# Attention, soft MoE and maxout on one core: another order of emission for all parts of a pair of heads

## The chip, the cores and the metric

The kernel runs on one core of a Trainium2 chip. The metric is the time of one execution on the device in microseconds, the median of several. The engines of a core run side by side, each through its own list of instructions in order: TensorE (PE in the profile; its weight loads are PEld), VectorE (DVE), ScalarE (ACT), GpSimd (POOL) and SyncE (SP), which here issues all DMA transfers.

## The reference

The inputs are q, k and v of 4 batches x 8 heads x 576 positions x 64, all in float32. Three layers follow each other:

```python
q_rot, k_rot = rotate(q), rotate(k)                    # rotary embedding
scores = q_rot @ k_rot.T / 8                           # 576 x 576 per head
attn = softmax(scores)                                 # exp(scores - row max) / row sum
x = (attn @ v) as [2304, 512]
logits = x @ phi                                       # 32 slots
slot_input = softmax(logits over all 2304 rows).T @ x  # soft mixture of experts
slot_out = relu(slot_input @ w1[e]) @ w2[e]            # 8 experts, 512 -> 1024 -> 512
y = softmax(logits over the slots) @ slot_out
h = max(y @ w1, y @ w2, y @ w3)                        # maxout, 512 -> 768
out = h @ w_out
```

## The kernel before

The 32 heads are worked through as 16 pairs (g = 0 to 15). A pair has nine units of up to 128 rows of scores: units 0, 2, 4, 6 belong to one head, 1, 3, 5, 7 to the other, and unit 8 holds the last 64 rows of both. Each unit runs through a chain over three engines. `emit_S` (PE, line 354; 342 in the first pair) computes the scores into one of three PSUM banks of the pool `ps_s`. `emit_max` (DVE, line 359) takes the row maximum. `emit_exp` (ACT, line 371) writes the exponentials to SBUF and their row sums. `emit_T` (PE, lines 380 to 386) transposes them back into the unit's bank, and `emit_Te` copies them out (ACT, lines 403 and 405; for unit 8 DVE, lines 408 and 411). Only then is the bank free for another S. So at most three units are on their way at once. Unit 8 has eight S matmuls, the others four.

`emit_PV` (PE, lines 430 and 433) multiplies them by v in two groups of five steps, PV0 (units 0 to 3) and PV1 (units 4 to 8), c0 to c4 each. Both accumulate in the one bank of the pool `ps_u`; `emit_u` reads it, first on ACT (called uhi here, line 442), then on DVE (ulo, line 440). `emit_x` (line 471) multiplies by the identity and by phi on PE, `emit_xe` (DVE, line 488) divides by the row sums of `emit_den`, `emit_lg` sums the logits. After each fourth pair `emit_end` adds the batch to the slot inputs (PE matmuls of lines 527, 541 and 556).

Ahead of S, a pair is prepared some two pairs earlier: loads of q, k and v (`load_qk`, `load_v`, `load_vr`), the rotation on POOL (`emit_rope`, parts q, k, r), transposes on PE into the bank of `ps_m` (`emit_qk`, called qk-q, qk-k, qk-r), a copy on ACT, the remainder of the split on DVE (`emit_lo`: lo-q, lo-k, lor), and DMAs within SBUF that lay the parts out (`emit_stack`, line 303, four DMAs each for q and k). Between all this runs a conversion of the last layer's weights from float64 bits to float32 (`convert`, 32 chunks in four steps each): DVE lines 610, 613, 615 and 618, with ACT lines 596 and 620 and POOL lines 622 and 624 in or after the fourth step. A `fill` is one step; `store` and `load_raw` on SP belong to the first step of a chunk. `emit_xr` splits phi, in the first pair.

The order is written out by hand, as numbers. Each part has a time in the table `TIMES`, counted in units; part X of pair g is put at 9 g + X. The events are sorted by that number, and each engine's list is the sorted list's part for that engine:

```python
for _, _, f, a in sorted(ev, key=lambda e: e[:2]):
    f(*a)
```

`first` replaces the times of the units in pair 0 and of the preparation of pair 1; `last` has those of the parts of pair 15 behind the units. In pair 15 the second PV group is split: a narrow part (y = 1, tile ul, the 64 last positions of both heads) and a wide one (y = 0).

The expert weights (32 loads of 1 MB, `load_w`, line 150) come into SBUF as space is free: ten during pairs 1 to 10, the other 22 behind the last conversion, where `swap` frees one pool after another (the working space of load, rotation and conversion; of the stacks; of S; of exp, T, Te and PV0; of PV1; of the rest) and later ones as the expert matmuls (line 742) have used the earlier ones.

Of the kernel before, what the change touches and what calls it, by code (L numbers as in the profile page):

```python
# [15 lines left out]

TIMES = {'PV0': [6.052698, 6.539022, 6.831161, 7.041179, 8.370574],
# [4 lines left out]
 'den': 9.045966,  # L24
 'dveT': [8],
 'end': [15.996553, 16.470809, 18.107722, 18.802385],
 'exp': [-0.675131, -0.916498, -1.127766, -0.304154, -0.913015, -1.011578, -0.953932, -0.243716, -1.040539],
 'fill': [-1.316643, 0.146837, 0.779834, 0.899125, 1.252142, 4.242488, 5.036954, 5.844713, 6.810021, 7.369609],
 'fill0': [-2.965317, 1.274402, 1.506862, 5.137451, -0.677174, 3.405875, 5.934943],
 'fillb': [0.263554, 0.659419, 1.262914, 4.782657, 7.03104],  # L30
# [3 lines left out]
           'exp': [-7.893717, -27.924269, -6.082201, -4.622187, -0.966764, -1.860446, -1.972664, 0.213131, -0.679221],  # L34
           'lok': -6.168845,
           'loq': -22.133635,
           'lor': -13.346412,
           'max': [-1.919995, 40.189116, -13.728982, -6.819962, -1.88512, -1.867328, -2.393284, -1.184347, -1.911995],
           'qkk': -8.826648,
           'qkq': -23.658995,  # L40
           'qkr': -13.35598,
           'stackk': -5.63826,
           'stackq': -11.947606},
 'h': [0, 0, 0.5, 1.5, 2, 2, 3.5, 4, 5.5, 5.0, 6.0, 6.5, 9.0, 10, 12.5, 18, 18.5, 24.0, 32.5, 40, 39, 44.5, 45, 51, 57, 58, 60.0, 68.0,
       71.5, 76.5],
 'hact': [[2, 2], [2, 5], [2, 1], [0, 5]],
 'last': {'PV1': [13.362323, 23.757612, 27.866613, 32.577903, 34.487854],
          'PV1b': [9.034314, 9.623589, 9.670028, 10.656968, 11.314749],
          'den': [12.059624, 7.065112],
          'end': [15.553272, 40.986824, 53.411692, 75.731423],  # L50
          'endb': [111.764265, 112.019026, 114.008368, 119.095903],
          'lg': [14.02684, 62.06959],
          'u1': [35.240849, 35.241849],
          'u1b': [29.443596, 31.049719],
          'warm': [[57.500286, 4], [57.655604, 4], [97.595993, 4]],
          'x': [11.566386, 42.509109, 34.56566],
          'xe': [[12.445342, 30.186802], [51.307524, 53.750567], [57.173325, 55.473275]]},
 'lg': [15.366289],
 'loadqk': -22.678765,
 'loadr': -22.34179,  # L60
 'loadv': -1.873124,
 'loadw': 15.022565,
 'lok': -7.015135,
 'loq': -11.030046,
 'lor': -9.491336,
 'max': [-1.11053, -1.080468, -1.701921, -1.209456, -0.992138, -1.336195, -0.990138, -0.989138, -1.184604],
 'onact': [1, 0, 0],
 'qkk': -8.083624,
 'qkq': -12.675556,
 'qkr': -10.180993,  # L70
 'ropek': -16.364586,
 'ropeq': -17.904547,
 'roper': -14.747196,
 'stackk': -6.992883,
 'stackq': -8.503989,
 'u0': [8.703314, 8.807017],
 'u1': [10.743395, 11.315174],
 'warm': [0, 0],
 'warm0': [24, 18, 5, 6],
 'warme': 3,  # L80
 'x': [11.5668, 12.630236, 13.065397],
 'xe': [12.623938, 14.727613, 13.993235],
 'xr': [-13.461787, -1.717465, -3.018039, 1.372009],
 'xu': [0, 1, 0]}


# [1 line left out]
def tile_kernel(ctx, tc, q, k, v, phi, w1, w2, g1, g2, g3, wo, rope, out):  # L88
# [45 lines left out]
    def slot(i, shape, dtype, name):  # L134

        if i == NW - 1:
            return late.tile(shape, dtype, tag="xy", name=name)
        pool = next(p for n, p in reversed(wpools) if i >= n)
        return pool.tile(shape, dtype, tag=f"w{i}", name=name)
# [248 lines left out]
    def emit_Te(n):  # L388
# [11 lines left out]
        src = s.rearrange("p b c -> p (b c)").rearrange("p (c i) -> p c i", i=128)  # L400
        copy = nc.vector.tensor_copy if j in TIMES["dveT"] else nc.scalar.copy
        if x == 0:
# [58 lines left out]
    def emit_x(g, ts):  # L461
# [4 lines left out]
        else:  # L466
            pool, tag = (ps_u, "u") if TIMES["xu"][ts[0] // 2] else (ps_m, "m")
            ps = pool.tile([128, 512], F32, tag=tag, name=f"x{g}_{ts[0]}")
# [38 lines left out]
    def warm(n, pool, tag, first):  # L507

        w = pool.tile([128, 2, 512], F32, tag=tag, name=f"warm{tag}") if first else run["warm"]
        run["warm"] = w  # L510
        for _ in range(n):
            nc.tensor.transpose(w[:, 0, 0:128], ident, ident)

    def emit_end(b, step, t0=0, t1=5):

        pool, tag = (ps_u, "u") if t0 else (ps_m, "m")
        if t0 and step in (2, 3):
            warm(TIMES["warme"], ps_s, "s", False)
        if step:
# [109 lines left out]

    WT = TIMES['warm']  # L630
    def emit_tail():
# [193 lines left out]
        def emit_h(k, f, part=(0, 1)):  # L825
# [14 lines left out]
            h = slot((6, 7, 13, 14)[i % 4], [128, 512], F32, f"hf{k}_{f}")[:, 0:n]  # L840
            if [k, f] in TIMES["hact"]:

# [38 lines left out]

        rows = sorted((t, i) for i, t in enumerate(TIMES["h"]) if i > 1)
        step = 0
# [215 lines left out]
```

## Time and profile before

| | |
|---|---|
| time, 3 runs | median 487.65 us (487.19 to 489.44) |
| span of the profiled execution | 486.8 us; the page gives no time of its own for it, the median lies 0.85 us above |
| PE, PEld, DVE, ACT, POOL busy | 466.3, 347.8, 345.4, 294.4, 282.6 us |
| pairs of heads | up to about 339 us, 18.6 to 21.3 us each |
| chain that ended last | PE 62%, DMA 13%, DVE 9%, ACT 8% of the span |
| DMA | 105.67 MB, mean 217 GB/s |

Read it from the stage and not from the shares: PE's busy time is modelled and includes what it waits inside an instruction, so the question is always which instruction starts late and who released it. A row of the timeline merges equal instructions that follow each other; the difference of two starts is what the first took, the printed length also holds the pipeline's depth. A row of the windows gives the stretch, its length, and the busy time with the number of instructions of PE, PEld, DVE, ACT and POOL in this order.

### The profile page before, as it was taken

The page shows a single profiled execution, that of the slowest core. Times are in us where ns is not written, and L with a number is a line of the kernel's source. Part 1 is how long each engine was busy: PE and PEld are TensorE (multiplying, and loading weights), DVE is VectorE, ACT ScalarE, POOL GpSimd, SP SyncE. Part 2 cuts the span into 40 slices and gives each one's busy share as a digit, 9 for nine tenths or more (in the row PEclk, how much of TensorE's full clock was granted, in tenths as well). Part 3 has the DMA queues.
Part 4 walks back from the last instruction along what each step waited for, and adds up shares of the span by engine and source line. Part 5 has one row for each costly group of instructions (what it writes and reads, how often), then busy time and mean ns, then how long its engine had stood idle before and what let it go on. Part 6 is the DMA issues. An engine that isn't in the chain of part 4 may idle for free.

```text
span 486.8 us, 9778 instructions
## 1 busy us (share of the span) xinstructions
PE 466.3 (96%) x3392; PEld 347.8 (71%) x3392; DVE 345.4 (71%) x663; ACT 294.4 (60%) x652; POOL 282.6 (58%) x374
## 2 busy tenths in 40 slices
PE   7899998999999999999999999998999899999996
PEld 7778676787777877868768687774334567888885
DVE  7878997987889898799988898466321367545520
ACT  2778887786978787788788688661111445322311
POOL 5998879777698796769976753011000287423420
PEclk9999999999999999999999999999999999999999
DMA  8679799979999998999989647999999501111111
GB/s 219 165 205 229 193 266 268 292 193 251 278 259 277 254 266 240 231 254 302 262 239 231 171 117 174 295 367 390 386 386 406 224 0 45 65 44 65 43 66 65
DMA packets 73121, 105.67 MB, mean 217 GB/s; under 512 B 12144, under 2 KB 41456, under 8 KB 72560
## 3 DMA queue, kind: packets, MB, share of 16 engines
q1 hardware_dynamic: 73072, 105.04, 73.8%
q8 instruction: 27, 0.44, 0.4%
q14 instruction: 22, 0.18, 0.1%
HBM read 66.98 MB, written 11.01 MB: 160 GB/s over the span
## 4 chain that ended last, share of the span: by engine, by line
PE 62%; DMA 13%; DVE 9%; ACT 8%; issue 3%; POOL 3%; SPq 2%; ACTq 0%; DVEq 0%; POOLq 0%
PE r L898 14%; PE s L354 11%; PE u L430 10%; PE s L380 9%; DMA qst<-qkt 3%; PE h L742 3%; DMA wof<-wod 3%; PE g L838 3%; ACT P L371 3%; PE u L433 2%; DMA kst<-qkt 2%; PE x L471 2%; DVE hf L847 2%; DMA wmd<-cv 2%; SPq L768 1%
## 5 line engine op out<-in xcount | busy, mean ns | idle before, releaser
L359 DVE TENSOR_REDUCE nm<-s 128x1 f32<-128x576 f32 x144 | 108.0, 750 | 18.4 <-PE s L354 15.7
L371 ACT ACTIVATE P<-s,nm 128x576 f32<-128x576 f32 x144 | 107.2, 745 | 14.6 <-DVE nm L359 13.1
L354 PE MATMUL s<-kst,qst 128*128 128x288 f32 x600 | 109.2, 312 | 3.0 <-ACT pt L403 1.6
L354 PEld LDWEIGHTS s<-kst,qst 128*128 128x128 f32 x600 | 84.3, 189 | 13.8 <-issue 6.8
L380 PE MATMUL s<-ident,P 128*128 128x128 f32 x576 | 90.9, 280 | 1.5 <-ACT P L371 1.3
L380 PEld LDWEIGHTS s<-ident,P 128*128 128x128 f32 x576 | 63.8, 140 | 25.1 <-ACT P L371 13.8
L898 PE MATMUL r<-wo,h 128*128 128x512 f32 x324 | 78.6, 391 | 0.4 <-ACT ob L862 0.2
L430 PE MATMUL u<-pt,vn 128*64 128x256 f32 (+1 forms) x512 | 72.0, 413 | 0.1
L898 PEld LDWEIGHTS r<-wo,h 128*128 128x128 f32 x324 | 60.3, 188 | 14.6 <-POOL h L858 0.9
L847 DVE TENSOR_REDUCE hf<-g 128x512 f32<-128x1536 f32 (+1 forms) x26 | 40.9, 1600 | 27.0 <-PE g L838 22.8
L858 POOL TENSOR_TENSOR h<-hf,h 128x512 fp32r<-128x512 f32 (+1 forms) x30 | 35.4, 1181 | 41.3 <-ACT h L857 41.1
L403 ACT COPY pt<-s 128x512 f32<-128x512 f32 x64 | 37.5, 587 | 26.7 <-PE s L380 25.5
L405 ACT COPY pt<-s 128x640 f32<-128x640 f32 x64 | 44.6, 697 | 8.0 <-PE s L382 7.6
L622 POOL TENSOR_TENSOR raw<-raw 128x384 f32<-128x384 f32 x32 | 27.1, 848 | 37.2 <-ACT raw L620 31.3
L430 PEld LDWEIGHTS u<-pt,vn 128*64 128x64 f32 x512 | 32.5, 136 | 22.4 <-issue 5.1
L857 ACT CAST h<-hf 128x512 fp32r<-128x512 f32 (+1 forms) x30 | 17.3, 578 | 48.2 <-DVE hf L847 42.8
L710 POOL TENSOR_TENSOR wo<-wof,wo 128x512 fp32r<-128x512 f32 x6 | 7.7, 1282 | 46.3 <-ACT wo L709 46.3
L624 POOL TENSOR_TENSOR cv<-cv,raw 128x384 f32<-128x384 f32 x32 | 32.7, 1023 | 2.5
L371 ACT ACTIVATION_READ_ACCUMULATOR P<-s,nm 128x1 f32 x144 | 28.9, 201 | 0.0
L615 DVE SCALAR_TENSOR_TENSOR cv<-raw,cv 128x384 uint32<-128x384 uint32 x32 | 27.5, 859 | 0.4
L471 PE MATMUL x<-xr,ut 128*128 128x256 f32 x160 | 26.4, 294 | 0.3 <-DVE qkt L297 0.3
L610 DVE TENSOR_SCALAR cx<-cv 128x384 f32<-128x384 f32 x32 | 17.5, 547 | 7.8 <-ACT cv L596 7.6
(363 smaller groups left out, 765.7 us busy)
## 6 DMA issues: line engine op xcount, KB each, us to landing
wt<-in_moe_w_dram SPq DMA_DIRECT2D x32, 1024.0 KB, 10.1
qst<-qkt SPq DMA_DIRECT2D x60, 288.0 KB, 6.2
raw<-in_moe_w_dram SPq DMA_DIRECT2D x24, 384.0 KB, 5.8
kst<-qkt SPq DMA_DIRECT2D x30, 160.0 KB, 5.1
wmd<-cv SPq DMA_DIRECT2D x24, 192.0 KB, 4.0
kst<-qkt SPq DMA_DIRECT2D x30, 144.0 KB, 5.2
vn<-in_v_dram SPq DMA_DIRECT2D x16, 256.0 KB, 6.8
wm<-wmd SPq DMA_DIRECT2D x4, 1024.0 KB, 14.2
```

Of the source, the lines that this page charges most:

```text
L354: nc.tensor.matmul(s[:, h, 0:288], l, r[:, 288 * h:288 * h + 288], start=(i == 0), stop=(i == len(todo) - 1))
L359: nc.vector.tensor_reduce(out=nm[n], in_=st[n][:, :, 0:288], axis=AX.XY, op=ALU.max, negate=True)
L371: nc.scalar.activation(out=dst.rearrange("p (h c) -> p h c", h=2), in_=s[:, :, 0:288], func=AF.Exp, bias=nm.pop(n), accum_out=acc)
L380: nc.tensor.transpose(s[:, 0, 128 * c:128 * c + 128], p[:, c0 + 128 * c:c0 + 128 * c + 128], ident)
L403: copy(out=o[:, 0:4, w + q0:w + q0 + 128], in_=src[:, 0:4, :])
L405: copy(out=o[:, 0:5, q0:q0 + 128], in_=src[:, 0:5, :])
L430: nc.tensor.matmul(u[r, 0:q1 - q0], vn[g][:, x, 64 * c:64 * c + 64], o[:, c, c0 + q0:c0 + q1], start=(c == 0), stop=False)
L471: nc.tensor.matmul(ps[:, 256 * i:256 * i + 256], utf[:, S * z + 128 * t:S * z + 128 * t + 128], xr[:, 0:hp + 2:hp + 1, :], start=(z == 0), ...
L624: nc.gpsimd.tensor_tensor(out=t3, in0=t3, in1=hf, op=ALU.add)
L847: nc.vector.tensor_reduce(out=h, in_=ps[:, :, 0:n].rearrange("p m n -> p n m"), axis=AX.X, op=ALU.max)
L858: nc.gpsimd.tensor_tensor(out=lo, in0=h, in1=hi.bitcast(F32), op=ALU.subtract)
L898: nc.tensor.matmul(p, a[:, s_], w, start=(z0 == 0 and z == 0), stop=(z0 == NF - 1 and z == 2))
```

## The change

Nearly all numbers of `TIMES` are others; no line of code beside the table is changed. The times of the tail (`h`, `hact`, the warming matmuls) are as they were.

```diff
- 'PV1': [9.241587, 9.242837, 9.546836, 10.367914, 10.622399],
- 'S': [-1.309708, -1.59755, -2.545633, -1.884619, -1.490997, -2.22163, -1.388557, -1.487997, -2.474781],
+ 'PV1': [9.714536, 9.714736, 9.714936, 9.715136, 9.715336],
+ 'S': [-1.74769, -1.606214, -2.189842, -1.701744, -1.95565, -2.08495, -1.560098, -1.975774, -3.300465],
...
- 'fill': [-1.316643, 0.146837, 0.779834, 0.899125, 1.252142, 4.242488, 5.036954, 5.844713, 6.810021, 7.369609],
+ 'fill': [-1.50987, 0.004675, 0.220815, 3.698955, 0.656176, 7.194923, 7.843254, 0.689867, 4.548494, 5.293259],
...
- 'first': {'S': [-3.975538, -2.669185, -21.686737, -6.89008, -7.669434, -2.602921, -2.632212, -1.578422, -2.027835],
+ 'first': {'S': [-3.975538, -2.669185, -57.562865, -12.285873, -18.031466, -15.122047, -2.687969, -5.348835, -8.984009],
...
- 'last': {'PV1': [13.362323, 23.757612, 27.866613, 32.577903, 34.487854],
-          'PV1b': [9.034314, 9.623589, 9.670028, 10.656968, 11.314749],
+ 'last': {'PV1': [25.832191, 26.930466, 26.930666, 26.930866, 26.931066],
+          'PV1b': [8.641384, 15.657113, 12.981078, 10.937847, 25.762469],
...
- 'loadv': -1.873124,
+ 'loadv': -4.720281,
```

What the two tables sort to, for a middle pair from the S of its unit 0 on (a prime marks the next pair; the numbers of the table are added to nine times the pair):

```
PE before   T7 S0' qk-r T8 PV0c4 S1' S2' T0' | PV1c0 c1 c2 T1' qk-k S3' PV1c3 c4 T2' S4' x01 S5' T3' x23 x4 T4' S6' T5' qk-q S7' S8' T6' PV0c0 c1 c2 c3
PE after    S0' T7 PV0c4 T8 qk-r S1' T0' S2' | PV1c0 c1 c2 c3 c4 qk-k T1' S3' T2' S4' x01 S5' T3' x23 x4 T4' S6' T5' S8' S7' qk-q T6' PV0c0 c2 c3 c1
DVE before  max0' Te8 lor ulo0 max1' den fill max2' fill fill fill max3' lo-k ulo1 max4' xe01 max5' fill xe4 max6' fill xe23 fill max7' lg fill max8' lo-q fill fill
DVE after   max0' fill Te8 lor ulo0 max1' max2' den fill fill fill fill ulo1 lo-k max3' max4' xe01 max5' fill xe23 fill max6' xe4 lg fill max7' max8' lo-q fill fill
SP before   fill stack-q fill fill fill stack-k fill load-qk fill fill load-w fill load-v fill fill
SP after    fill stack-q fill fill fill fill stack-k load-qk load-v fill fill load-w fill fill fill
```

In the first pair PE's order was S2, qk-q, T0, T1, qk-r, S3, S4, T2, qk-k, T3, S5, S6, T4, T5, qk-q, S7, T6, S8, PV0; it becomes S2, qk-q, T0, T1, qk-r, T2, S4, S5, S3, T4, qk-k, T5, S8, T3, S7, S6, T8, qk-q, PV0 c0, c2, c3, T6, PV0 c1. On DVE max2 moves ahead of lo-q, and on ACT and DVE the first conversion step ahead of exp1. In the last pair the narrow PV1 (ul), x01, the wide PV1, x4 and x23 were interleaved with the first part of the end step; they become: narrow PV1, all of the wide PV1, x01, x23, x4, then the matmuls of the end step.

## Rows read from the trace of the kernel before

**Rows 1.** The page's busy line: us, share of span, instructions, by engine.
```profile
PE 466.3 (96%) x3392; PEld 347.8 (71%) x3392; DVE 345.4 (71%) x663; ACT 294.4 (60%) x652; POOL 282.6 (58%) x374
```

**Rows 2.** Windows, one per pair: length, busy us (instructions) per engine, PEclk, DMA share, GB/s.
```profile
67.89:88.49 20.60, 19.23 (x143) 14.63 (x142) 17.29 (x37) 15.72 (x35) 15.21 (x22) 1.00 0.98 278
...
207.38:225.99 18.61, 18.61 (x143) 14.62 (x142) 17.88 (x37) 15.44 (x35) 14.57 (x20) 1.00 0.98 258
...
285.20:303.86 18.66, 18.51 (x138) 14.26 (x137) 16.85 (x36) 14.89 (x34) 7.52 (x11) 1.00 0.55 135
```

**Rows 3.** Windows of the end of the loop and the expert layers, same columns.
```profile
309.00:327.00 18.00, 17.47 (x146) 13.35 (x146) 10.67 (x25) 11.89 (x28) 1.70 (x5) 1.00 1.03 368
...
330.00:360.00 30.00, 27.96 (x253) 11.13 (x256) 13.84 (x36) 5.75 (x12) 2.21 (x6) 0.94 1.04 388
```

**Rows 4.** Timeline of SyncE's issues (start, length, what, count), the weight loads.
```profile
305.30 53.98 SPq L150 DMA_DIRECT2D wt<-in_moe_w_dram  x22
```

**Rows 5.** Timeline of PE in a middle pair: start us, length, instruction, tiles, count.
```profile
209.25 0.66 PE L380 MATMUL s<-ident,P 128*128 128x128 f32 x4
...
210.50 0.60 PE L380 MATMUL s<-ident,P 128*128 128x128 f32 x4
210.93 0.38 PE L386 MATMUL s<-ident,P 128*128 128x128 f32 x2
211.25 0.65 PE L433 MATMUL u<-pt,vr 128*64 128x256 f32 x4
211.83 1.55 PE L354 MATMUL s<-kst,qst 128*128 128x288 f32 x8
213.22 0.60 PE L380 MATMUL s<-ident,P 128*128 128x128 f32 x4
213.75 1.84 PE L430 MATMUL u<-pt,vn 128*64 128x320 f32 x12
215.51 0.66 PE L380 MATMUL s<-ident,P 128*128 128x128 f32 x4
...
216.47 0.78 PE L354 MATMUL s<-kst,qst 128*128 128x288 f32 x4
217.18 0.76 PE L430 MATMUL u<-pt,vn 128*64 128x320 f32 x4
218.41 0.66 PE L380 MATMUL s<-ident,P 128*128 128x128 f32 x4
```

**Rows 6.** Timeline of DVE in the same pair: max0, Te8, ulo0.
```profile
210.63 0.75 DVE L359 TENSOR_REDUCE nm<-s 128x1 f32<-128x576 f32 x1
211.42 0.69 DVE L408 COPY pt<-s 128x512 f32<-128x512 f32 x1
...
212.94 0.42 DVE L440 TENSOR_TENSOR ut<-u,ut 128x256 fp32r<-128x256 f32 x1
```

**Rows 7.** SyncE's issues of the k stack, and the page's row on them.
```profile
218.40 3.36 SPq L303 DMA_DIRECT2D kst<-qkt  x4
...
kst<-qkt SPq DMA_DIRECT2D x30, 144.0 KB, 5.2
```

**Rows 8.** Timeline of the first pair: pauses of PE in brackets, first PV, a conversion.
```profile
17.33 0.30 PE L255 MATMUL tq1r<-ident,rot 128*128 128x128 f32 x1 [0.54 <-DVE qkt L294]
...
25.98 0.66 PE L380 MATMUL s<-ident,P 128*128 128x128 f32 x4 [0.61 <-ACT P L371]
...
30.02 1.95 PE L430 MATMUL u<-pt,vn 128*64 128x256 f32 x16
...
19.25 0.56 ACT L596 ACTIVATE cv<-raw 128x384 f32<-128x384 f32 x1
```

**Rows 9.** Timeline of PE: T7 of the last pair, and the first expert matmuls.
```profile
323.83 0.66 PE L380 MATMUL s<-ident,P 128*128 128x128 f32 x4
...
339.01 3.46 PE L742 MATMUL h<-wt,sitxr 128*32 128x512 f32 x16 [0.38 <-DVE sitxr L648]
```

**Rows 10.** The instructions of line 615: min/median/max ns, first and last start, form.
```profile
L615 DVE SCALAR_TENSOR_TENSOR cv<-raw,cv x32: 543/685/1661, 21.0 to 295.1; 128x384 uint32<-128x384 uint32 x32
```

More of the change, by code (lines that the diff above doesn't have):

```diff
@@ L15 @@
 PSUM = bass.MemoryType.PSUM
-TIMES = {'PV0': [6.052698, 6.539022, 6.831161, 7.041179, 8.370574],
[4 rows of a table removed]
- 'den': 9.045966,
- 'dveT': [8],
- 'end': [15.996553, 16.470809, 18.107722, 18.802385],
- 'exp': [-0.675131, -0.916498, -1.127766, -0.304154, -0.913015, -1.011578, -0.953932, -0.243716, -1.040539],
- 'fill': [-1.316643, 0.146837, 0.779834, 0.899125, 1.252142, 4.242488, 5.036954, 5.844713, 6.810021, 7.369609],
- 'fill0': [-2.965317, 1.274402, 1.506862, 5.137451, -0.677174, 3.405875, 5.934943],
- 'fillb': [0.263554, 0.659419, 1.262914, 4.782657, 7.03104],
[3 rows of a table removed]
[L34 to L43, printed above, removed]
+TIMES = {'PV0': [5.801776, 6.839926, 6.445569, 6.498141, 7.668547],
[4 rows of a table added]
+ 'den': 8.951732,
+ 'dveT': [8],
+ 'end': [15.497906, 16.108947, 17.14458, 18.345512],
+ 'exp': [-1.044649, -0.910808, -1.522529, 0.124466, -0.868834, -1.18186, -0.877027, -0.086048, -0.254473],
+ 'fill': [-1.50987, 0.004675, 0.220815, 3.698955, 0.656176, 7.194923, 7.843254, 0.689867, 4.548494, 5.293259],
+ 'fill0': [-30.054912, 0.899973, 6.984371, 1.128841, 6.083735, -24.514505, 3.75481],
+ 'fillb': [0.441804, 1.055732, 6.580648, 5.294359, 8.826661],
[3 rows of a table added]
+           'exp': [-7.893717, -28.325435, -27.06825, -4.232094, -13.249875, -11.591257, 0.373057, -3.768565, -4.968302],
+           'lok': -11.523888,
+           'loq': -27.777461,
+           'lor': -19.969723,
+           'max': [-1.919995, 40.189116, -57.386677, -8.481998, -16.937649, -13.096599, -1.405152, -4.950458, -6.128992],
+           'qkk': -15.528871,
+           'qkq': -35.560199,
+           'qkr': -26.716406,
+           'stackk': -6.619004,
+           'stackq': -13.642629},
  'h': [0, 0, 0.5, 1.5, 2, 2, 3.5, 4, 5.5, 5.0, 6.0, 6.5, 9.0, 10, 12.5, 18, 18.5, 24.0, 32.5, 40, 39, 44.5, 45, 51, 57, 58, 60.0, 68.0,
@@ L46 @@
  'hact': [[2, 2], [2, 5], [2, 1], [0, 5]],
- 'last': {'PV1': [13.362323, 23.757612, 27.866613, 32.577903, 34.487854],
-          'PV1b': [9.034314, 9.623589, 9.670028, 10.656968, 11.314749],
[L49 to L54, printed above, removed]
-          'warm': [[57.500286, 4], [57.655604, 4], [97.595993, 4]],
-          'x': [11.566386, 42.509109, 34.56566],
-          'xe': [[12.445342, 30.186802], [51.307524, 53.750567], [57.173325, 55.473275]]},
@@ L58 @@
- 'lg': [15.366289],
- 'loadqk': -22.678765,
- 'loadr': -22.34179,
- 'loadv': -1.873124,
[L62 to L66, printed above, removed]
- 'onact': [1, 0, 0],
[L68 to L76, printed above, removed]
@@ L77 @@
- 'u1': [10.743395, 11.315174],
+ 'last': {'PV1': [25.832191, 26.930466, 26.930666, 26.930866, 26.931066],
+          'PV1b': [8.641384, 15.657113, 12.981078, 10.937847, 25.762469],
+          'den': [46.371958, 13.658914],
+          'end': [86.705504, 154.608803, 155.902892, 167.034198],
+          'endb': [161.192031, 167.881351, 205.956702, 254.918022],
+          'lg': [69.752909, 138.112981],
+          'u1': [39.877973, 62.274113],
+          'u1b': [39.514245, 45.969331],
+          'warm': [[57.500286, 4], [57.655604, 4], [97.595993, 4]],
+          'x': [51.329358, 90.550427, 115.608145],
+          'xe': [[51.96689, 91.769692], [101.442818, 180.501963], [121.887548, 243.803931]]},
@@ new lines @@
+ 'lg': [14.136701],
+ 'loadqk': -22.887155,
+ 'loadr': -20.170925,
+ 'loadv': -4.720281,
+ 'loadw': 15.560719,
+ 'lok': -7.719845,
+ 'loq': -12.028476,
+ 'lor': -9.222222,
+ 'max': [-1.210263, -1.15714, -2.116904, -1.297388, -1.264612, -1.316647, -1.447118, -1.464186, -2.434375],
+ 'onact': [1, 0, 0],
+ 'qkk': -7.789306,
+ 'qkq': -12.472911,
+ 'qkr': -9.673959,
+ 'ropek': -14.779118,
+ 'ropeq': -18.027128,
+ 'roper': -12.327438,
+ 'stackk': -5.235867,
+ 'stackq': -8.793576,
+ 'u0': [8.382799, 8.82357],
@@ L78 @@
+ 'u1': [9.735097, 10.136409],
  'warm': [0, 0],
@@ L80 @@
  'warme': 3,
- 'x': [11.5668, 12.630236, 13.065397],
- 'xe': [12.623938, 14.727613, 13.993235],
- 'xr': [-13.461787, -1.717465, -3.018039, 1.372009],
+ 'x': [11.564881, 12.8471, 13.197909],
+ 'xe': [12.278459, 12.934187, 13.78606],
+ 'xr': [-44.589697, -21.755635, -16.961095, -4.056977],
  'xu': [0, 1, 0]}
```

8 rows, old and new, of the table TIMES are left out of this document.

## The prediction

> **What bounds the kernel now.** I read the busy shares of the page first: the matrix engine (PE) is busy for 96% of the span, VectorE (DVE) for 71% [rows 1]. Both figures mix stages, so I cut the span into pairs of heads, from the first PV matmul of one pair to that of the next [rows 2]. There the reader is to see three things. A good pair takes 18.61 us, and PE does not pause in it. DVE has 17.88 us busy of the same 18.61, so only 0.73 us of it is free. And the pairs differ: 20.60 us is the worst of those with the same PE instructions. By this cut five pairs lie at 18.61 to 18.67 us, and the other six without end-of-batch work exceed 18.65 by 0.4 to 1.95 us, about 5 us in sum.
>
> Then I looked at the end. From 309 to 360 us the DMA engines are busy throughout and move 368 to 388 GB/s [rows 3]: weights stream while PE finishes the last pair and runs the expert layers. SP issues 22 weight loads from 305.30 on, over 54 us [rows 4], each when its space comes free. So the kernel's end follows the time at which the loop over pairs lets this stream start and feeds it; what comes after it is not touched by the change.
>
> **The change part by part.** It moves numbers only. Every engine executes the same instructions; no operation, byte or buffer is added or removed. So the terms are waits, and PE's cost of going in and out of PV.
>
> *Middle pairs, PE.* From S0 of the next pair on, the new table gives S0, T7, PV0 c4, T8, qk-r, S1, T0, S2, all five PV1, qk-k, T1, S3. Before it was T7, S0, qk-r, T8, PV0 c4, S1, S2, T0, PV1 c0 to c2, T1, qk-k, S3, PV1 c3 and c4. That stretch ran from T7 at 209.25 to T2 at 218.41, 9.16 us [rows 5]. The new sum from the same rows: T7 and S0 1.14 (209.25 to 210.50, less 0.11 for qk-r), and 0.11 to go into PV, as T0 took 0.53 ahead of PV1 against 0.42 for its four transposes alone; PV0 c4 0.58; T8 0.64, six at 0.106; qk-r 0.11; S1 0.60, half of the 1.39 for S1 and S2 less a 0.2 us pause between the two; T0 0.42; S2 0.71, what S3 took ahead of PV1 c3; PV1 2.94, twenty at 0.147, as twelve took 1.76; T1 and qk-k 0.96; S3 0.58, the mean of a plain S at 0.56 and one behind another kind. That is 8.79 us, 0.37 less: PE goes into PV one time fewer, and S1 and S2 no longer stand together.
>
> *Middle pairs, the new wait.* PV1 overwrites the accumulator that PV0 left, so it waits for ulo0 on DVE, whose order keeps Te8, lor, ulo0 in a row. Before, T8 is issued ahead of PV0 c4, through at 211.14 (two at 0.106 from 210.93); ulo0 ends at 213.36, 2.22 us later [rows 6], and PV1 came 2.61 us later: no wait. Now T8 comes behind PV0 c4, and from its end PE has only qk-r, S1, T0 and S2, 0.11 + 0.60 + 0.42 + 0.71 = 1.84 us. That leaves a wait of 0.38 us per pair; behind the waiting PV1 stand qk-k, T1 and S3, and for S3 waits the next max. Net: -0.37 + 0.38, which I take as zero. Bounds: -0.37 if Te8 and lor come early enough, +0.50 if DVE stretches (rival 3); over the 14 pairs, -5.2 to +7.0 us.
>
> *S8 ahead of S7, qk-q behind both.* S8 is the long one with eight matmuls, so Te5 is covered better; but it now wants the bank of unit 4 right behind T5, and the cover lost for Te4 is qk-q, four transposes, 0.42 us. I cost it at nothing; bounds -0.3 to +0.42 per pair, inside those above.
>
> *Loads and conversion steps.* On SP's queue the k stack still comes behind the conversion steps of the pair's start, and the v loads move up behind it. Before, the four k stacks are issued from 218.40 to 221.76 and take 5.2 us to land [rows 7], so they are there at about 227, 1.4 us ahead of the S0 that needs them (209.78 + 18.61). I keep that margin, and cost all these moves at -0.8 of the 5 us of excess, a sixth of it: the order of the conversion steps among themselves stays nearly what it was, so most of these pauses stay. Bounds -4 to +3 us.
>
> *First pair.* PE pauses six times between 17 and 26 us, by 0.54 at the first and 0.61 at the last, 2.7 us in all [rows 8]: qk-r behind lo-q, an S that waits for its bank, T5 behind a late exp. The new order puts max2 at once behind max1 on DVE, runs S4 and S5 ahead of S3 and T4, and brings S8 and T8 forward, so that Te8 is done long before PV1 and the new wait does not arise. Against it, a conversion step of 0.56 us on ScalarE (ACT) now stands ahead of exp1, and S8 must wait for Te5, some 0.9 us by the same durations. Following the chain so, PV0 starts near 28.7 instead of 30.02, with T8 done earlier and T7 later; the gain is between 1.4 and 2.0 us, and I take 1.7. Bounds +1.5 (exp1 late by 0.6, and the whole stall at S8) to -2.7 (all pauses gone).
>
> *Last pair.* T8 stands behind PV0 c4, which delays the narrow PV1, and x01 stands behind the wide PV1 (20 matmuls at 0.117, 2.3 us), with the whole softmax chain of the end behind it. So the expert matmuls, 15.2 us behind the start of the last T7 before [rows 9], come about 2.9 us later. What hides this is the stream: a load of 1 MB takes 2.7 us at 388 GB/s, and the queue holds several. I cost it at zero; if the cover is short, up to +1.5.
>
> *Sum.* 486.8 - 1.7 - 0.8 + 0 + 0 = 484.3 us of span. The median of the runs shown, 487.65, lies 0.85 above the span of the profiled execution; so the forecast is 484.3 + 0.85 = 485.1 us by the median.
>
> **The rivals.** *Rival 1, the merge pays.* Te8 comes early on DVE, the wait does not appear, and the 0.37 us per pair are real: 14 x 0.37 = 5.2, with 1.7 and 2 us of the excess, gives 487.65 - 8.9 = 478.8. For it: PE is the engine that does not pause [rows 2]. Against it: the 2.22 us chain above.
>
> *Rival 2, hidden anyway.* The pairs run at the pace of transfers: both in the 18.61 and in the 20.60 us pair the DMA engines are busy for 0.98 of the time [rows 2]. Then what PE gains in the first pair is lost where a stack or the stream of weights is late, and the time stays at 487.6. Against it: the pair from 285.20 on, with a DMA share of 0.55, took 18.66 us as well [rows 2].
>
> *Rival 3, VectorE becomes the bound: slower.* Place: between max0 and Te8, where DVE now waits for T8 some 0.5 us that were 0.04 before (211.38 to 211.42). DVE has 0.73 us free per pair; once its other waits exceed 0.2 us, every further one lengthens the pair. Price: 0.5 us x 14 = 7, less the first pair's 1.7, plus 1 at the end, no other gain: 494. For it: 17.88 of 18.61, and a conversion step, line 615, that takes 0.54 us or 1.66 [rows 10]. The Trainium skill's page SBUF — State Buffer, section Who interferes with whom, says that a VectorE instruction with two SBUF inputs is blocked for the whole of a GpSimd instruction that reads SBUF; line 615 has two such inputs, the trace agrees in that it spreads so far, and with five steps bunched beside the q rotation this rule speaks for the rival.
>
> **How the numbers follow.** About 0.5%, 2.4 us, is what can be told from no change here. Forecast 485.1, its own range 482 to 488.5: chance 0.40. Rival 1, 478.8: 0.22. Rival 2, 487.6: 0.18. Rival 3, 494: 0.20. Faster (under 485.2): all of rival 1 and a little over half of the forecast, 0.45. Within: the rest of the forecast and most of rival 2, 0.33. Slower: rival 3 and the edge of rival 2, 0.22. The range takes in rival 1 and most of rival 3, 477.5 to 493.
>
> **What would show it.** Right: first PV of the kernel at about 28.7; good pairs still near 18.6; PV1 as one row of 20 matmuls with up to 0.4 us of pause before it, ended by ulo0 (line 440); expert matmuls (line 742) some 18 us behind the last T7, with the DMA engines still busy throughout. Good pairs at 18.3 would be rival 1, pairs at 19 with DVE without a gap rival 3. Wrong altogether: a pause of over 1 us per pair at S1 or S8, that is, a bank given to them that is not free, or DMA engines that fall idle between 340 and 360.

## The result, and the profile after

The changed kernel takes 493.81 us (median of 4, 491.59 to 495.81) against 488.15 us for the kernel before, measured beside it (4 runs, 487.19 to 489.44): a ratio of 1.0115, 95% interval 1.0082 to 1.0148. It is slower by some 5.6 us, above the forecast of 485.1 and just outside the range's upper end. The profiled execution is the slowest of the four: it took 495.81 us, with a span of 494.0. The ratios leave out executions far off the others of the same kernel, above all one of e2 that took 1553.73 us.

The page's busy line, as in [rows 1]:

```profile
PE 465.7 (94%) x3392; PEld 354.0 (72%) x3392; DVE 346.7 (70%) x663; ACT 296.1 (60%) x652; POOL 279.1 (56%) x374
```

PE works as long as before in a span 7.2 us longer, so PE pauses more. The pairs, with the columns of [rows 2]:

```profile
87.11:105.59 18.48, 18.25 (x142) 14.67 (x142) 15.28 (x33) 15.29 (x36) 13.52 (x21) 1.00 1.02 238
...
207.35:226.76 19.41, 18.26 (x143) 14.70 (x142) 17.10 (x36) 15.74 (x36) 14.80 (x22) 1.00 1.00 256
226.76:249.71 22.95, 20.44 (x143) 16.25 (x142) 18.77 (x38) 16.32 (x38) 16.61 (x23) 0.93 1.01 258
...
325.83:346.84 21.01, 16.64 (x162) 11.26 (x161) 9.94 (x35) 4.53 (x13) 2.98 (x10) 0.84 1.00 368
```

A good pair is 18.48 us, 0.13 better than the 18.61 of [rows 2]. But the pair from 207.35 takes 19.41, the next one 22.95, and from the last pair's first PV to the expert matmuls 21.01 us pass, where it was 17.1 before (321.95 to 339.01).

What PE waited for in the loop, 30 to 325 us, is in the next two fences: total us, times, longest. First after:

```profile
PE s L380 <- ACT P L371: 4.2, 8, 1.4
PE s L354 <- issue: 3.5, 3, 1.2
PE s L354 <- DVE pt L411: 2.3, 11, 0.3
PE s L354 <- ACT pt L405: 1.3, 3, 0.7
```

and before, in the same stretch:

```profile
PE s L354 <- ACT pt L403: 1.6, 3, 1.3
PE s L380 <- ACT P L371: 0.6, 2, 0.3
PE s L354 <- DVE pt L411: 0.6, 2, 0.4
PE s L354 <- ACT pt L405: 0.5, 2, 0.2
PE x L471 <- DVE qkt L297: 0.3, 1, 0.3
```

The sums are 11.3 and 3.6 us. Of the 11.3, 5.8 are two kinds of wait that the prediction didn't have in this place: S matmuls (line 354) that wait for the second half of Te8 (line 411), and three of 1.2 us that the view calls "issue", its word for a wait for nothing that it can name. Another 4.2 are T behind a late exp. The timelines show each.

**The bank of S8.** The timeline of PE behind T8 in the changed kernel, in the pairs from 207.35 and 226.76:

```profile
211.58 0.38 PE L386 MATMUL s<-ident,P 128*128 128x128 f32 x2
211.80 0.27 PE L255 MATMUL tq11r<-ident,rot 128*128 128x128 f32 x1
213.23 0.76 PE L354 MATMUL s<-kst,qst 128*128 128x288 f32 x4 [1.15 <-issue]
...
231.23 0.78 PE L354 MATMUL s<-kst,qst 128*128 128x288 f32 x4
231.85 0.60 PE L380 MATMUL s<-ident,P 128*128 128x128 f32 x4
232.67 0.76 PE L354 MATMUL s<-kst,qst 128*128 128x288 f32 x4 [0.23 <-DVE pt L411]
233.37 2.37 PE L430 MATMUL u<-pt,vn 128*64 128x320 f32 x16
```

and DVE's Te8 in the first of them, in its two parts:

```profile
212.07 0.69 DVE L408 COPY pt<-s 128x512 f32<-128x512 f32 x1 [0.78 <-PE tq11r L255]
212.68 0.45 DVE L411 COPY pt<-s 64x64 f32<-64x64 f32 x2
```

In the second of these pairs S1 runs at once and S2 waits until Te8 has emptied unit 8's bank; start to start, S2 comes about 0.4 us late (0.82 behind T0, whose four transposes take 0.42). In the first, S1 starts at 213.23, when Te8 ends at 213.13: there S1 was given unit 8's bank. The addresses in the built program say the same: S1 has unit 8's bank in pairs 3, 8 and 10, the three with the "issue" wait, and unit 7's in the other middle pairs. So 11 pairs lose 0.3 to 0.5 us at S2, three lose 1.32 us at S1, about 8 us together. PV1, where the prediction put the wait, comes without a pause.

The kernel before has the same wait, only shorter. By its built program S2 takes unit 8's bank in every pair from 1 to 15, and in the pair of [rows 5] S2 starts just behind Te8's second part:

```profile
212.03 0.45 DVE L411 COPY pt<-s 64x64 f32<-64x64 f32 x2
```
```profile
212.62 0.76 PE L354 MATMUL s<-kst,qst 128*128 128x288 f32 x4
```

**The store of a conversion.** SP's store of a finished chunk, from the timeline of pair 10:

```profile
230.77 0.34 SPq L590 DMA_DIRECT2D wmd<-cv  x1
```

The view of the tile cv from 228 to 246 us gives its two stores' time from issue to landing:

```profile
DMA to landing us min/median/max: 6.2/6.7/7.2
```

And ACT's timeline in the same pair:

```profile
234.81 0.56 ACT L620 ACTIVATE raw<-raw 128x384 f32<-128x384 uint32 x1
238.03 0.55 ACT L596 ACTIVATE cv<-raw 128x384 f32<-128x384 f32 x1 [2.66 <-POOL raw L622]
238.48 0.72 ACT L371 ACTIVATE P<-s,nm 128x576 f32<-128x576 f32 x1
```

Line 596 is the absolute value of the next chunk; it writes the one of two tiles cv that the store issued at 230.77 was still reading. The store landed 7.2 us later, at 237.96, and line 596 starts at 238.03. (The releaser printed, POOL's line 622, ended at 237.82; the landing is the later one, and in the built program line 596 waits for its own chunk's load, for that store and for line 624 of the chunk before the last, not for line 622.) All six pauses of over 0.15 us ahead of line 596 in this profile, and all five in that of before, end 0.07 to 0.11 us behind the landing of such a store. Behind line 596 on ACT, in order, stand exp2, uhi1, the copy of qk-k and Te1. PE in the same stretch:

```profile
237.17 0.77 PE L354 MATMUL s<-kst,qst 128*128 128x288 f32 x4
239.35 0.66 PE L380 MATMUL s<-ident,P 128*128 128x128 f32 x4 [1.41 <-ACT P L371]
240.74 1.18 PE L354 MATMUL s<-kst,qst 128*128 128x288 f32 x4 [0.73 <-ACT pt L405]
```

Four S matmuls now last 1.18 in place of 0.77, for behind these pauses the granted clock is 0.50, that is 1.2 of 2.4 GHz, as the windows show:

```profile
241.00:243.00 2.00, 2.00 (x10) 2.00 (x10) 1.43 (x3) 1.20 (x4) 1.91 (x2) 0.50 1.05 266
243.00:245.00 2.00, 2.00 (x14) 1.98 (x13) 1.79 (x4) 0.96 (x3) 0.00 (x0) 0.66 1.07 244
```

How much this costs differs between executions: in e1 below, whose loop is the same, the same store landed after 6.1 us and this pair took 20.49 us.

**First and last pair.** PE in the first pair, beside [rows 8], and T7, the softmax step and the expert matmuls of the last, beside [rows 9]:

```profile
16.52 0.66 PE L380 MATMUL s<-ident,P 128*128 128x128 f32 x4 [0.72 <-ACT P L371]
...
24.24 1.85 PE L342 MATMUL s<-kst,qst 128*128 128x288 f32 x12 [1.32 <-ACT pt L405]
...
29.51 1.51 PE L430 MATMUL u<-pt,vn 128*64 128x256 f32 x12
...
327.71 0.66 PE L380 MATMUL s<-ident,P 128*128 128x128 f32 x4
...
339.10 0.37 PE L541 MATMUL e<-dg,xy 32*128 32x32 f32 x2 [1.70 <-DVE dg L535]
...
346.84 3.55 PE L742 MATMUL h<-wt,sitxr 128*32 128x512 f32 x16 [0.38 <-DVE sitxr L648]
```

The first PV comes 0.5 us earlier, the expert matmuls 19.1 us behind T7 where it was 15.2. And the weight stream falls idle for a while, by the windows of the changed kernel:

```profile
344.00:348.00 4.00, 3.06 (x33) 1.14 (x29) 1.75 (x8) 0.00 (x0) 1.14 (x4) 0.50 1.04 386
348.00:352.00 4.00, 4.00 (x32) 0.94 (x28) 2.95 (x6) 0.74 (x1) 0.00 (x0) 0.73 0.65 238
```

Between 348 and 352 the DMA engines have a share of 0.65, in the next 4 us 0.91; before, it was 1.05 throughout 340 to 356. The last transfer of w_out lands at 392.1 us instead of 386.5, and the last products start at 394.03 instead of 387.63.

### The profile page after: what moved, and what is told of

It is laid out like the page before. It is cut to its first block, busy times and chain, and to the rows that moved or that the text cites. A ratio compares the mean times of both kernels' runs of the same rounds, so it can differ in the third digit from the quotient of the medians.

```text
span 494.0 us, 9745 instructions
## 1 busy us (share of the span) xinstructions
PE 465.7 (94%) x3392; PEld 354.0 (72%) x3392; DVE 346.7 (70%) x663; ACT 296.1 (60%) x652; POOL 279.1 (56%) x374
## 4 chain that ended last, share of the span: by engine, by line
PE 62%; DVE 15%; DMA 9%; ACT 5%; issue 4%; POOL 2%; SPq 1%; ACTq 0%; DVEq 0%; POOLq 0%
PE r L898 15%; PE s L354 10%; PE u L430 8%; PE s L380 7%; DMA wt<-in_moe_w_dram 4%; DVE nm L359 3%; PE h L742 3%; PE g L838 3%; PE ops L758 3%; DMA kst<-qkt 2%; PE u L433 2%; ACT P L371 2%; DVE cv L615 2%; PE x L471 2%; PE tq L801 2%
## 5 line engine op out<-in xcount | busy, mean ns | idle before, releaser
L359 DVE TENSOR_REDUCE nm<-s 128x1 f32<-128x576 f32 x144 | 105.4, 750 | 17.4 <-PE s L354 12.4
L354 PEld LDWEIGHTS s<-kst,qst 128*128 128x128 f32 x600 | 84.5, 190 | 17.5 <-issue 5.8
L380 PE MATMUL s<-ident,P 128*128 128x128 f32 x576 | 89.6, 278 | 5.0 <-ACT P L371 4.9
L898 PE MATMUL r<-wo,h 128*128 128x512 f32 x324 | 79.7, 395 | 0.4 <-ACT ob L862 0.2
L380 PEld LDWEIGHTS s<-ident,P 128*128 128x128 f32 x576 | 65.7, 141 | 15.7 <-ACT P L371 9.3
L430 PE MATMUL u<-pt,vn 128*64 128x256 f32 (+1 forms) x512 | 68.9, 410 | 0.1
L430 PEld LDWEIGHTS u<-pt,vn 128*64 128x64 f32 x512 | 34.2, 136 | 23.8 <-issue 2.9
L471 PEld LDWEIGHTS x<-xr,ut 128*128 128x128 f32 x160 | 21.9, 193 | 0.7 <-issue 0.4
```

Source lines behind the costliest of these rows:

```text
L354: nc.tensor.matmul(s[:, h, 0:288], l, r[:, 288 * h:288 * h + 288], start=(i == 0), stop=(i == len(todo) - 1))
L359: nc.vector.tensor_reduce(out=nm[n], in_=st[n][:, :, 0:288], axis=AX.XY, op=ALU.max, negate=True)
L380: nc.tensor.transpose(s[:, 0, 128 * c:128 * c + 128], p[:, c0 + 128 * c:c0 + 128 * c + 128], ident)
L430: nc.tensor.matmul(u[r, 0:q1 - q0], vn[g][:, x, 64 * c:64 * c + 64], o[:, c, c0 + q0:c0 + q1], start=(c == 0), stop=False)
L471: nc.tensor.matmul(ps[:, 256 * i:256 * i + 256], utf[:, S * z + 128 * t:S * z + 128 * t + 128], xr[:, 0:hp + 2:hp + 1, :], start=(z == 0), ...
L898: nc.tensor.matmul(p, a[:, s_], w, start=(z0 == 0 and z == 0), stop=(z0 == NF - 1 and z == 2))
```

## The experiments

Each ratio is to the kernel before, run on the same chip beside it; the interval is 95%. A percent is 4.9 us. The runs were spread over several chips, where the kernel before had medians of 487.0 to 489.1 us, so differences between two runs are taken from the ratios and not from the medians; such a difference is known to about 2 us. The profiled execution of the run is used for the rows.

### One part back or alone

```diff
  # e1: the new table with the old 'last'; 'den' of the narrow group at 8.6
  # e2: the old table with the new 'last'
  # e3: the new table with the old 'fill' and 'fillb'
  # e4: the old table with the new 'first', 'fill0' and 'xr'
```

> The new table with the last pair's entries of the old one (one entry, the narrow group's denominators, is set to 8.6 so that it stays behind exp8). Theory A, the last pair: its longer PE chain (from its first PV to the expert matmuls 21.0 us against 17.1) starves the weight stream; then this kernel falls by 3 to 4.5 us from the new one's 493.8, to 489.5 to 491, and the expert matmuls come about 17 us behind the pair's first PV. Theory B, the conversion's store: a step on ACT that waits for a store of the conversion delays a pair in the middle (pair 10: 22.95 us, with the clock at half speed behind it) and is the main part; then the last pair is hidden by the stream and the time stays at 493 to 494.

Measured: 490.23 us, ratio 1.0027 (0.9996 to 1.0057), that is 0.9% below the changed kernel. From the first PV of the last pair to the expert matmuls 17.95 us pass. As theory A said in size; theory B's pair 10 was 20.49 in this profile with a wait of 1.41 on ACT, so a spread between executions is mixed into the difference.

> The old table with the new entries of the last pair alone. Theory A: 3 to 4.5 us above the kernel before, 491 to 492.5, with the expert matmuls 3 to 4 us later and the last transfer of w_out landing 2 to 3 us later. Theory B: within 1 us of the kernel before, 487 to 489.

Measured: 490.06 us, ratio 1.0028 (0.9999 to 1.0057), some 1.4 us. The expert matmuls come 19.56 us behind the pair's first PV, 2.5 more than before. A cost at the edge of the noise, and less than theory A's 3 to 4.5. The wait for a store is there in the old loop too: in this profile ACT waited 2.46 us for one, and the pair from 223.74 took 21.57 us.

> The new table with the old times of the conversion steps of pairs 1 to 15 (fill and fillb). Theory B: the pair of 22.95 us falls to 19 to 20, the clock stays up there, and the kernel is at 489 to 490.5 (the last pair's share stays). Theory A: 493 to 494, since the waits for the store only move to other pairs (they sum to 6.3 us on ACT in the old kernel and 3.4 in the new).

Measured: 508.64 us, ratio 1.0386 (1.0328 to 1.0444). Both theories missed, by 15 us or more. PE's waits in the loop:

```profile
PE s L380 <- ACT P L371: 10.0, 15, 1.6
PE s L354 <- ACT pt L405: 4.8, 9, 0.7
```

In the old table exp8 stood ahead of the steps at -1.63 and -1.32; in the new one it is emitted behind them, so a step that holds ACT now holds exp8, T8, Te8 and S1. The mechanism of theory B is there and larger (line 596 pauses for 7.9 us in this profile, 5.8 in that of the changed kernel); that the old times would cure it was wrong. Times of conversion steps are worth something only together with the order around them.

> The old table with the new order of the first pair alone (its units, the preparation of pair 1, its conversion steps, the split of phi). As predicted for the first pair: 1.7 us below the kernel before. By the new kernel's trace the first PV came only 0.5 us earlier: then 0 to 0.7 us below, 487.4 to 488.2, and if later pairs run at the pace of transfers, no difference.

Measured: 487.70 us, ratio 1.0002 (0.9976 to 1.0028): nothing. The first PV was at 29.63, 0.39 earlier, and the next pair took 19.79 us in place of 18.65.

### T8, S8 and the merged PV1

```diff
  # e5, on the new table
- 'exp': [..., -0.254473]     'T': [..., 0.272783]
+ 'exp': [..., -0.43]         'T': [..., -0.4]
  # e7: e5 with the last pair as in e1
  # e6, on the new table
- 'S': [..., -1.975774, -3.300465]
+ 'S': [..., -1.975774, -2.97]
  # e8, on the old table
- 'PV1': [9.241587, 9.242837, 9.546836, 10.367914, 10.622399]
+ 'PV1': [9.241587, 9.242837, 9.546836, 9.5469, 9.547]
```

> The new table with T8 of each middle pair put between T7 and PV0 c4, as it stood before (exp8 is renumbered so that it stays ahead of it; its place on ACT is the same). Theory S, the bank of S8: in the new table the S that takes S8's bank waits for Te8, in 11 pairs S2, by 0.3 to 0.5 us each, in pairs 3, 8 and 10 S1, by 1.32 us each: 8 us in sum against 5.2 that the merged PV1 gives. With T8 0.58 us earlier the waits at S2 go and those at S1 fall to 0.7: 4 to 6 us below the new kernel, 488 to 490. Theory D, the loop runs at the pace of transfers and of VectorE: the pauses only move to PV1 or to the next S, and the time stays within 1 us of 493.8.

Measured: 489.74 us, ratio 1.0057 (1.0035 to 1.0078), 2.8 us below the changed kernel. Good pairs are 18.17 us, and no S2 waits for line 411 any more; the three S1 that take unit 8's bank still start 0.7 us late, start to start (the view puts 0.4 us of each down to PE's line 255; in the pair from 206.05, Te8 ends at 211.08 and S1 starts at 211.18). So these waits went as theory S said. The gain is less, and the waits for exp stayed:

```profile
PE s L380 <- ACT P L371: 4.1, 6, 1.1
```

> As the first run of this call, and the last pair in the old order too. If the two costs add: 4 to 6 us below the kernel that has the last pair put back alone (490.2), so 484 to 486, below the kernel before by 3 to 5 us. Theory D: 489 to 491.

Measured: 488.15 us, ratio 1.0020 (0.9993 to 1.0047). The costs do not add here: by the ratios it is only 0.3 us below e1, inside the intervals. In its profile the pair from 66.99 takes 22.24 us at a granted clock of 0.92; there ACT waited 3.05 us for a store.

> The new table with S8 back behind S7 (nothing else moved). In the listing of this kernel S1 takes S8's bank in pairs 3 and 8 alone, no more in pair 10. Theory S: one pause of 1.3 us less, another of 0.4 more, so 0 to 1 us below the new kernel. If S8 ahead of S7 is worth something by itself (T5 and Te5 covered better), this kernel is slower by up to 14 x 0.4 = 5.6 us.

Measured: 498.93 us, ratio 1.0238 (1.0208 to 1.0267), 6 us above the changed kernel, the upper end of the second alternative. The row says why:

```profile
PE s L354 <- ACT pt L405: 4.7, 14, 0.7
```

In every pair an S waits 0.4 us, start to start, for a bank that Te frees. So S8 ahead of S7 is worth 0.4 us a pair in the new order. The expectation is wrong on pair 10: by the built program S1 takes unit 8's bank in pairs 3, 8 and 10 here too, and the trace has three waits of 1.2 us, as in the changed kernel.

> The old table with the five PV1 steps of a middle pair in one row behind T0 (c3 and c4 drawn forward past T1, qk-k and S3). By the term of the prediction, a PV entry of PE is worth up to 0.37 us a pair: 14 x 0.37 = 5.2 us below the kernel before, pairs of 18.3 in place of 18.6. Rival: T1, qk-k and S3 come 1.2 us later and max3 with them, so VectorE, which has 0.73 us free, idles: 0 to 5 us above.

Measured: 495.11 us, ratio 1.0175 (1.0146 to 1.0203), 8 us slower, beyond the rival's 5. The pair that answers to the 18.61 of [rows 2], and the waits:

```profile
210.54:230.20 19.66, 19.14 (x143) 14.81 (x142) 17.98 (x37) 15.38 (x35) 14.58 (x20) 1.00 0.94 256
```
```profile
PE s L354 <- ACT pt L405: 4.5, 15, 0.3
```

The rival had the place nearly: T1 comes later, Te1 with it, and S4 waits for its bank in each pair. In the new order, e9 merges PV1 too, without such a wait.

### The wait for the store taken away

Line 596 now writes the tile cx, which is free by then; the clamp works in it, and cv is taken one step later. Instructions, bytes and space are the same. Two other things change with it: by the built programs S1 then gets unit 7's bank in pairs 3, 8 and 10 of the new table too, and the clamp on VectorE takes longer (see e10).

```diff
-            t0s[i] = one.tile([128, CW], F32, tag="cv", name=f"cv{i}", bufs=2)
-            nc.scalar.activation(out=t0s[i].rearrange("p (t a) -> p t a", t=3), in_=..., func=AF.Abs)
+            t0s[i] = one.tile([128, 3, 129], F32, tag="cx", name=f"cx{i}")[:, :, 0:128]
+            nc.scalar.activation(out=t0s[i], in_=..., func=AF.Abs)
...
-            t1 = one.tile([128, 3, 129], F32, tag="cx", name=f"cx{i}")[:, :, 0:128]
-            v.tensor_scalar(out=t1, in0=t0, ...)
+            v.tensor_scalar(out=t1, in0=t1, ...)
             yield
+            t0 = one.tile([128, CW], F32, tag="cv", name=f"cv{i}", bufs=2)
```

> T8 first and the last pair in the old order, as in the run of 488.15, and besides: a conversion's absolute value is written to the tile cx and clamped there, and the tile cv is taken only in the next step, so that ACT no longer waits for the store of the chunk before the last to land. Same instructions, bytes and space. Theory C, the store: ACT waits of 1 to 3 us in pairs 2, 6, 9 and 10, which make T2 or S wait in turn, are the rest of the excess; they go, and the kernel comes to 482 to 484.5. Theory D, the pace of transfers: the time lost shows up at another wait (a stack, a load), 487 to 488.5.

Measured: 483.70 us (482.15 to 489.16), ratio 0.9938 (0.9906 to 0.9971). As theory C said, and faster than both kernels, by 0.6% and 1.8%. Its profile is of the slowest of its twelve executions. A good pair in it, in which PE does not pause, and the next one:

```profile
242.94:260.97 18.03, 18.03 (x143) 14.67 (x142) 15.26 (x33) 14.37 (x33) 13.96 (x22) 1.00 1.00 232
260.97:286.07 25.10, 21.81 (x193) 17.56 (x192) 18.66 (x43) 16.97 (x40) 14.63 (x21) 0.93 0.81 191
```

In the second an S waits 1.55 us for a k stack to land, among other pauses; in e13's profile the same pair takes 20.90 us.

> The kernel before with the conversion's tile changed in the same way and nothing else. Theory C: its waits for the store on ACT sum to 6.3 us in the trace (1.53 the longest), partly covered; 2 to 5 us below the kernel before. Theory D: within 1 us of it.

Measured: 490.88 us, ratio 1.0070 (1.0041 to 1.0098): slower, against both theories. The clamp (line 610 of the kernel before, 608 here) now reads and writes one tile, and it takes longer; before, and here:

```profile
L610 DVE TENSOR_SCALAR cx<-cv x32: 526/550/555, 19.8 to 293.9; 128x384 f32<-128x384 f32 x32
```
```profile
L608 DVE TENSOR_SCALAR cx<-cx x32: 400/713/1253, 19.8 to 295.6; 128x384 f32<-128x384 f32 x32
```

That is 23.0 us of VectorE in place of 17.5; why it is longer no run here shows. In the first pair the clamp takes 1.09 us, and the max, the exp and the T behind it come 1.2 us later. PE pauses 1.44 us there, and from 26 to 29 us the granted clock is 0.50, where it was 1.00 before. So the first PV is at 32.15, 2.1 us late; e15 below avoids that.

> The new table whole, with the conversion's tile changed in the same way. In the listing S1 now gets S7's bank in pairs 3, 8 and 10 too, so that the three pauses of 1.32 us become 0.4, and ACT no longer waits for the store. Theory C: 4 to 7 us below the new kernel's 493.8, 487 to 490. If it stays over 492, the last pair and the waits at S2 make the whole loss.

Measured: 489.79 us, ratio 1.0033 (1.0009 to 1.0058), 4.0 us below the changed kernel. PE's waits in the loop fall from 11.3 to 6.1 us, and the "issue" ones are gone:

```profile
PE s L354 <- DVE pt L411: 2.8, 12, 0.3
PE s L380 <- ACT P L371: 2.7, 7, 0.7
```

The two effects of the edit, no wait for the store and S1 never in unit 8's bank, are not separated by this run.

> The best kernel so far (483.7: the conversion's tile changed, the last pair in the old order, T8 ahead of PV0 c4) with T8 back behind PV0 c4, as the new table has it. No S waits for a store now, so the waits for S8's bank are alone. Theory S: good pairs 18.5 in place of 18.03, S2 waits 0.4 in 14 pairs: 14 x 0.45 = 6 us above the best kernel, 488 to 490. Theory D, pace of transfers: T8's place had made only 0.3 us where the last pair was old: 484 to 485.

Measured: 485.94 us, ratio 0.9983 (0.9962 to 1.0004), 2.2 us above e9, though the two intervals overlap a little. The good pairs are as expected:

```profile
165.65:184.15 18.50, 18.28 (x142) 14.73 (x141) 15.10 (x32) 14.69 (x34) 12.96 (x19) 1.00 0.88 231
```

but the total is between the theories: in pairs that wait elsewhere as well, T8's place costs nothing on top (those from 205.26 and 224.09 take 18.83 and 19.38 us, in e13's profile 18.83 and 19.40).

> The best kernel so far with the new order of the last pair. Theory A: expert matmuls 3 us later behind the pair's first PV, the queue of weights runs dry for a while between 340 and 360, the first of the last products 2 to 3 us later: 485.5 to 487. As the prediction had it, hidden by the stream: within 1 us of 483.7.

Measured: 485.90 us, ratio 0.9978 (0.9956 to 1.0000), 2 us above e9, as theory A said, though the two intervals overlap a little. The expert matmuls come 20.31 us behind the pair's first PV, in e9 17.21, and DMA falls to 0.85 for a while:

```profile
340.00:344.00 4.00, 4.00 (x40) 0.96 (x32) 2.10 (x4) 1.25 (x2) 0.00 (x0) 0.97 0.85 300
```

> The old table with the new first pair (487.7 in its run) and the conversion's tile changed. The old table with the tile alone came out 0.7% slower, and its trace has the first PV 2.1 us later, which this first pair should take away. Theory C: the loop's waits for the store are then gone and the kernel is 2 to 4 us below the kernel before, 483.5 to 485.5. If it stays at 487 to 488.5, the old loop hid these waits, and they cost only where the new order put the step ahead of exp8, Te1 or exp1 on ACT.

Measured: 489.06 us, ratio 1.0031 (1.0006 to 1.0055), no gain over e4's 1.0002. Line 596's waits in the profile of before, 4.4 us by its pauses (the expectation's 6.3 counts every gap ahead of it), are gone, but the clamp takes VectorE 5.4 us more than in e4, and S waits 2.2 us for line 411 where it waited 0.7 in e4. So this edit gives the old order nothing on balance; what the store alone cost it is not shown.

## Why the prediction was wrong

**The step that failed first: the middle pairs.** "-0.37 + 0.38, which I take as zero." The gain exists: without the waits good pairs are 18.17 (e5) and 18.03 us (e9) against 18.61, 0.44 to 0.58 less, and e6 shows that some 0.4 of that hangs on S8 ahead of S7, which I had cost at nothing with a gain of 0.3 as the bound; what the merged PV1 gives by itself no run separates. The wait exists too, with nearly the size worked out (0.38; 0.3 to 0.5 at S2). But its place was wrong: I followed Te8 to lor, ulo0 and PV1, and did not ask which S takes unit 8's bank. Te8 is asked for earlier, at S2, and in three pairs at S1, where it costs 1.32. The hint was in my own term for S1, "less a 0.2 us pause between the two": that pause is S2 waiting for unit 8's bank in the kernel before, and I took it off instead of asking what it was. My sign of "wrong altogether", a pause of over 1 us at S1 for a bank that is not free, came in three pairs. T8's place alone is worth 2.2 us (e12 to e9) to 2.8 (the changed kernel to e5), between e1 and e7 only 0.3.

**The step that failed most: the conversion steps.** "The order of the conversion steps among themselves stays nearly what it was", -0.8 us. I treated the steps as DVE work of 0.55 us and never followed their ACT part to what it waits for. The new table puts four steps of a pair between 0.005 and 0.69, on ACT ahead of exp2, uhi1 and Te1, and line 596 comes sooner behind the store that must free its tile: of 30 such stores the middle one had 5.9 us to land before and 4.8 after, and 7 had under 5 us before, 16 after. The stores took up to 7.2. ACT's pauses there sum to 5.8 us in the profile of the changed kernel, 6.0, 8.4 and 8.6 in those of e1, e5 and e7, against 4.4, 4.0 and 0.9 with the old loop (before, e2, e4); the 3.4 in the expectation of e3 was too low. The distance is not all: in pair 10 it is 4.4 us before and 4.6 after, and there the store landed after 5.3 and 7.2 us, for a reason that stays open. The edit of the tile gives 2.1 us (e1 to e12) to 4.0 (the changed kernel to e11) in the new order, the better bank of S1 in three pairs included, and nothing in the old (e15). So my upper bound of +3 for this step was about its size, and -0.8 had the wrong sign.

**The last pair.** Predicted 2.9 us later, measured 3.9 (from 15.2 to 19.1 us behind T7); the cover, "I cost it at zero; if the cover is short, up to +1.5", was short: 1.4 us in the old order (e2), 2 in the best (e13), 4.3 between the changed kernel and e1, where the intervals are wide. Its sign I had named: DMA engines that fall idle between 340 and 360. Added to the lateness is the clock, 0.50 in 340 to 348, behind the 1.70 us of idle PE before 339.10 and others.

**The first pair.** -1.7 us predicted, -0.5 measured at the first PV. S8's wait for Te5, put at 0.9, is 1.32, and exp1 behind the conversion step makes T wait 0.72 at 16.52. The 0.4 us that e4 gained did not live beyond the next pair.

**Sum.** Put back one at a time into e9, T8's new place costs 2.2, the last pair 2.0, the tile 4.0 (e7 to e9): 8.2 us, where all three together are 8.6 (1.0115 less 0.9938, 1.77%). The changed kernel, e1, e5, e7, e9, e11, e12 and e13 are the eight combinations of these three, so each can be read four times: T8's place costs 0.3 to 2.8 us, 2.0 in the mean, the last pair 1.8 to 4.3, 2.6 in the mean, the tile 2.1 to 4.0, 3.5 in the mean. The means add up to 8.1 us, and the forecast, 2.5 us below the kernel before, missed by as much. With the three put right (e9) the new table is 3.0 us faster than the kernel before; without the edit of the tile (e7) it is not. So the change had a gain and buried it under three waits. That e9 lies near the forecast is luck: its gain is in the middle pairs, which I had at zero.

**The rivals.** Rival 1 (478.8) came true in the length of e9's good pairs, 18.03, not in the time. Rival 2: the first pair's gain did vanish (e4); but a good pair of 18.03 at a DMA share of 1.00 says that transfers don't set the loop's pace, though a late stack or store holds single pairs up (e9's 25.10 us, pair 10). Rival 3 forecast 494, the time that came and more than my range's end of 493, and its place was right: in the pair from 207.35 DVE stands idle 0.78 us ahead of Te8, waiting for T8. But DVE is not the bound: it is busy for 17.10 us of that pair's 19.41, and for 15.28 of the good one's 18.48. What the late Te8 holds up is an S on PE. The rule cited for it is seen once more in pair 10:

```profile
234.56 1.28 POOL L223 TENSOR_TENSOR rot<-rot,qn 128x512 f32<-128x512 f32 x1
```
```profile
234.70 1.56 DVE L615 SCALAR_TENSOR_TENSOR cv<-raw,cv 128x384 uint32<-128x384 uint32 x1
```

By the Trainium skill's page SBUF — State Buffer, section Who interferes with whom, a VectorE instruction with two SBUF inputs is blocked while GpSimd holds the shared port; the trace agrees: line 615 ends 0.42 us behind POOL's instruction, where it takes 0.54 alone. It was not what ended last here: the store landed at 237.96.

## What to carry to other kernels

When transposes, copies and matmuls share a few rotating buffers, work out for each new order which instruction is next to take each buffer, and price a wait at the first that asks for it, not at the consumer of the data. A side job that is cut into steps between the main work carries its own waits onto the in-order engine where its step stands: ask of each step what it waits for (here the landing of a store, 2 to 7 us) and what is queued behind it. And parts of such an order are not worth something each by itself: e3 and e6 put one part of the change back and came out 2.7 and 1.2% slower than with it. An edit that is to take one wait away can change more than that: here the tile's edit also changed banks and made an instruction longer.

## What was not expected of the hardware

A conversion's store issued at 277.76 us in the profile of before landed 2.0 us later, one issued at 230.77 in that of after 7.2 us later, in a pair with a DMA share of 1.01. Pauses of PE of 1.41 and 0.73 us ahead of 239.35 and 240.74 were followed by a granted clock of 0.50 from 241 to 243 and 0.66 to 245, though PE did not pause again from 240.74 to 245. In the pair from 207.35, with its one pause of 1.15 us, it stayed at 1.00. A clamp on VectorE took 526 to 555 ns from one tile to another and 400 to 1253 ns within one tile (before, e10).
